# Linear attention and gated MLP, two layers on one core: queries kept token-major and turned by DMA, MLP norm from sums taken with the residual

## The chip, the core and the metric

The kernel runs on one core of a Trainium2 chip. The metric is the device time of one execution in microseconds, the median of the runs shown. PE is the matmul engine, DVE the vector engine, ACT the activation engine, POOL the GpSimd engine, and SP the engine whose queue issues nearly all DMAs.

## What is computed

The input is 2048 tokens of 512 features in bf16. Two layers follow each other with the same weights: attention, then MLP, each added to the residual x. The norm has no weights.

```
x = x + A(layernorm(x)); x = x + B(layernorm(x)); and both once more

A: q, k, v = split(x @ wqkv) into 32 heads of 16
   pq, pk  = q @ w_phi[h], k @ w_phi[h]
   phi     = concat(softmax(p), softmax(-p))            # 32 features a head
   kv, z   = sum over tokens of phi_k^T v, and of phi_k
   o       = (phi_q @ kv) / (phi_q . z + 1e-6);  result = o @ wo
B: gate = relu(x @ W_gate); up = x @ W_up; result = (gate * up) @ W_down     # F = 1376
```

## The kernel before

Tokens lie in 16 tiles of 128 rows, and x stays in SBUF as bf16 from the first load to the last store. w_phi is folded into the key and query weights at the start (`fold`), so PE computes pk and pq directly.

**Keys.** Per tile, `norm_A` takes mean and variance on DVE (L810, L811), ln and exp on ACT for the reciprocal root (L818, L820), and scales on DVE (L825). `turn` transposes the tile into `xnTA`, by DMA from SP (L787) or, for a few tiles, by PE matmuls and a copy. `Keys.begin` computes pk (L849) and v (L855), exp of +pk and -pk on ACT (L852), and sums over 16 features on DVE (L860). `Keys.finish` and `scale` turn sums into factors by ln and exp (L867, L870) and multiply two halves of 512 on DVE or GpSimd (L879). `kvz` accumulates the 65-column products of all 16 tiles in PSUM (L896). `build` then writes the masked matrix R (L918, L924).

**Queries.** `queries` computes pq feature-major, four tiles at a time (L937), and ACT writes exp(+pq) and exp(-pq) into `Eq` (L941), which is used as it lies, without a softmax sum. `attend` multiplies each of the eight groups by R with 144 columns (L955): numerators and denominators, and also the softmax sums, so that DVE can weigh both signs (L971 to L985). The result o is turned (L787 or L797), projected (L992) and added to x (L1001; L997 for the first two tiles, with the row sum).

**MLP.** `mlp` handles blocks of 1, 2 or 4 tiles: statistics (L810), centring (L1022, L1018), a turn into `xnTB`, gate and up products (L1068, and L1044 for the last 96 features), relu on ACT (L1072), a copy of up to SBUF on ACT or DVE (`evac`, L752 or L753), their product on DVE (L1076), down products (L1101), and the scaled residual (L1108).

**Order.** `op` only records operations. `plan` then places them in time by written costs, due numbers (`DUE`) and free buffers, and each engine runs its own operations in that order. `PLACE` chooses between two engines where an operation has an `alt`. Each engine's queue is in order, so an instruction that waits holds up all behind it. `idle` inserts filler matmuls on PE (L746) in gaps of the first layer's keys. Layers overlap: the keys of layer 1 start while the MLP of layer 0 still runs.

Of the kernel before, what the change touches and what calls it, by code (L numbers as in the profile page):

```python
# [8 lines left out]
P = 128  # L9
# [14 lines left out]
GE = HB * (DH + 2)  # L24
# [12 lines left out]
class Op:  # L37
    __slots__ = ("eng", "occ", "lat", "due", "emit", "deps", "takes", "uses", "start", "end", "left",
                 "then", "ready", "name", "n", "move", "spent", "port", "follow", "behind", "alt", "twin")

    def __init__(self, eng, cost, due, emit, deps=(), takes=(), uses=(), name="", move=0, port=False,
                 follow=(), alt=None):
        self.eng, (self.occ, self.lat) = eng, cost
# [35 lines left out]
FRESH = 0.77  # L79


def plan(ops):
# [11 lines left out]
    lanes = [0.0] * LANES  # L94
    open_ = {e: [o for o in ops if o.eng == e and not o.left] for e in HOP}
    order = []
    while len(order) < len(ops):
# [34 lines left out]
        if o.eng == "PE":  # L132
            warm = t + COLD if warm is None else warm
            if t < warm:
                occ, lat = 2 * occ, lat + occ
        if o.move:
            queue = max(t + 1400, queue) + o.move * (FRESH if queue < 9000 else 1.0)
            lat = max(lat, queue + 600 - t)
            lanes = lanes[1:] + [t + lat + HOP["SP"]]
        o.start, o.end, o.spent = t, t + lat, occ  # L140
# [48 lines left out]
def mm(n, cols):  # L189
    t = n * (cols / 2.4 + 2.5)  # L190
    return t, t + 170


def act(n, sbuf=False):
    return (n / 1.2 + (275 if sbuf else 64), n / 1.2 + (385 if sbuf else 170))
# [6 lines left out]
def dve(n, rate=1, more=56):  # L202
    t = n / rate / 0.96 + more
    return t, t + 98
# [7 lines left out]
RESSUM = (750, 850)  # L212
RLN, REXP = ((150, 265), (203, 318)), ((145, 262), (198, 315))
SUMS = (8 * 32.5, 8 * 32.5 + 170)
STATS = (592, 692)
SUM16 = (1140, 1225)
CENTRE, SCALE = (240, 350), (315, 410)
FILL = 216
XPOSE, XPOSE_LOADS = (1245, 3600), (1245, 3600)
RATE = 250.0  # L220


def dma(nbytes):
    return 530, 2000 + nbytes / RATE


class K:
# [9 lines left out]
    "1101000110000001001100001000100000000000010001111000011000010001110001000000000000011100100010111111"  # L237
    "1111000010110100000100000010000001100000011001011000011111100010000100001101010000001001111011010000"
    "1111100110100000010110000100000010100000010011011010100001000001001010001111110011001101111011000111"
    "1"  # L240
# [3 lines left out]
SUM_ON_PE, SPLIT, SUMMED = False, False, 2  # L244
PAIRN, PAIRK = 4, T
# [5 lines left out]
    124840698555718, 124252925051631, 124840698555715, 125332623046249, 125332623046237, 125332623044945,  # L251
    124563716811943, 124651474002544, 125330408190868, 125332623046304, 124563716811957, 126266507667699,
    125634454115563, 126229628066192, 121775727240306, 126167001450013, 126167001450460, 127129188121561,
    127129188120464, 127094235901023, 126466639653490, 130976565015723, 126315242830809, 126026073780216,
    127094235902555, 127129188121381, 126296162928321, 126296162928067, 124164240787164, 125426364192401,
    125402334135098, 125572680463274, 125519371767392, 125974726071829, 125750504763376, 125579757280012,
    125111116517781, 125262546662859, 123870973169851, 125479091639646, 125519634893654, 125402750569735,
    125720420032606, 126315242829367, 126115429498044, 125777194724969, 125402334135128, 125288327727618,
    125426364192382, 125079834957741, 125262546664085, 125297196294117, 125083742970748, 125572680463271,
    125682458895960, 125340531910116, 125650771760537, 124924227899641, 125375805988896, 125375805988747,  # L260
    125222585690632, 124164240787379, 125079834952887, 125682458896453, 125073457285470, 124441555417783,
    125262546664362, 124559450906168, 125312265963603, 125309490505260, 125650771760388, 125521196029889,
    125302414876135, 125288971855969, 125302414876075, 125319036718893, 125310924577113, 125301244472799,
    125319889098234, 125304622980711, 124441555417022, 124696086271192, 125037102060107, 125289095968268,
    125310342882178, 125097433264852, 123938863413234, 125098635011495, 125302414877679, 125298443103361,
    125302414877834, 125345179807080, 125281974922696, 125170893464912, 125310924577844, 125298773455122,
    124760528650159, 125079834956090, 124164240787032, 125519634912639, 125297196294120, 125289095970570,
    125112530384860, 124947956071454, 125087041208877, 125295339242047, 125295339242044, 125310342881683,
    125302414876836, 125563590222055, 124550413597701, 125170893460583, 125310439811694, 125310924578485,
    125310342891023, 125079834956128, 125059086062919, 125340531910042, 125288971857093, 124938480631522,  # L270
    125016964293686, 125288327733509, 125223398503866, 125345179804453, 125223398503371, 125223398503413,
    128002429020973, 125310342881575, 125004873625443, 125004873624115, 125304250990101, 125307858833262,
    126406478372943, 124715538660738, 125381551257299, 125298773455119, 125309931740009, 125034120871986,
    125223398503145, 124934003878247, 124920547621783, 125117660356287, 125304250989589, 125381551258296,
    125724846491348, 125381551257440, 125381551255756, 124974964922671, 125098650067446, 125291692659804,
    125289095968030, 125289095968469, 125345179805242, 125288327732492, 125098635010687, 125281974923160,
    125307858833059, 125223398502787, 125307858834522, 125140858237361, 126040889629027, 125223398503832,
    125364446854524, 125252231261123, 125381551257841, 125304250990712, 125381551257935, 125172912230709,
    124370185364736, 125108599924050, 125310339518705, 125302251176246, 125291692659817, 116464344164560,
    124922363544296, 125116688267329, 125108599923765, 125310109452139, 125303189236999, 125098650066178,  # L280
    125111066291136, 125026249417504, 125310339519068, 125302251175868, 125301748943397, 125307858834419,
    125262656080157, 125307858833334, 125307858831723, 125281974922936, 125016007547146, 125096908962168,
    125140858236352, 126184070097670, 126789461067573, 124985972327150, 126493631750672, 125298443105832,
    125108599921161, 125095405692172, 124194527561572, 123915330190996, 125076395401661, 125296253501352,
# [321 lines left out]
def kernel(  # L606
# [17 lines left out]
    def psum(name, n):  # L624
        return Pool([pp.tile([P, 512], F32, name=f"{name}{i}") for i in range(n)])
# [3 lines left out]
    def x_of(t):  # L629
        return X[t // C][:, t % C, :]  # L630
# [113 lines left out]
    def idle(n):  # L744
        for _ in range(n):
            nc.tensor.matmul(wps.t[:], lhsT=zero[:, 0:P], rhs=zero[:], start=True, stop=True)  # L746
# [473 lines left out]
```

## Time and profile before

| | |
|---|---|
| time, median of 3 runs | 383.84 us (383.63 to 384.19) |
| span of the profiled execution | 382.02 us |
| its own time | not given apart; median less span is 1.8 us |
| PE, DVE, ACT, POOL busy | 371.5, 311.1, 215.0, 41.9 us |
| first attention matmul of layer 0, layer 1 | 54.4, 237.5 us from the start |
| DMA | 22.83 MB, mean 60 GB/s; 188 to 232 GB/s in most slices of the first 50 us |

The instructions on an engine overlap a little at their ends, so a group's mean times its count is more than its busy time. The chain of waits gives the pace of matmuls that follow each other without a gap. A DMA's time to landing counts from its issue.

### The profile page before, as it was taken

To read this page: it belongs to the slowest core of one execution; us is meant where nothing else is said; L and a number is where in the kernel's file an instruction comes from. 1 tells how busy PE (TensorE), PEld (TensorE's weight loads), DVE (VectorE), ACT (ScalarE), POOL (GpSimd) and SP (SyncE) were. 2 spreads that over 40 slices of the span, in tenths; PEclk is the share of its full clock that TensorE was granted. 3 is DMA by queue.
4 is the path that set the end of the run, shared out by engine and by line. 5 is a ranking of instruction groups with operands and counts; after the bars stand their busy time and mean duration, and the time that the engine had idled before them with its cause. 6 is when DMAs were issued, how large, how long until landed. Compare 5 with 4: busy or idle time off the path is not lost.

```text
span 382.0 us, 7622 instructions
## 1 busy us (share of the span) xinstructions
PE 371.5 (97%) x2787; PEld 224.4 (59%) x2832; DVE 311.1 (81%) x798; ACT 215.0 (56%) x554; POOL 41.9 (11%) x44
## 2 busy tenths in 40 slices
PE   7999998999989999999999999999999999999996
PEld 4545456967545445554656654696855544467575
DVE  7999999999999989983694677999998976763334
ACT  6999989636445316772455679984526412243040
POOL 0276710000200000230020124000000000000000
PEclk9999999999999999999999999999999999999999
DMA  8497720222221321211200100013322221020110
GB/s 232 122 205 219 188 89 2 52 58 62 57 56 41 44 54 40 45 23 27 45 6 15 22 8 1 2 36 70 77 44 70 57 56 56 14 62 16 41 50 29
DMA packets 60869, 22.83 MB, mean 60 GB/s; under 512 B 52672, under 2 KB 59808, under 8 KB 60832
## 3 DMA queue, kind: packets, MB, share of 16 engines
q1 hardware_dynamic: 60416, 21.95, 24.9%
q8 instruction: 22, 0.36, 0.4%
q10 hardware_dynamic: 416, 0.39, 0.4%
q14 instruction: 15, 0.12, 0.1%
HBM read 7.91 MB, written 2.10 MB: 26 GB/s over the span
## 4 chain that ended last, share of the span: by engine, by line
PE 77%; DVE 17%; DMA 2%; issue 2%; ACT 1%; DVEq 0%
PE b L1068 31%; PE b L1101 17%; PE b L855 5%; PE b L849 5%; PE b L992 5%; PE b L937 5%; PE q L955 3%; PE b L1044 2%; PE q L896 2%; DMA xnTA<-xn 2%; DVE pr L980 1%; DVE bstA L810 1%; DVE bstB L810 1%; DVE sk L860 1%; DVE N L753 1%
## 5 line engine op out<-in xcount | busy, mean ns | idle before, releaser
L1068 PE MATMUL b<-xnTB,wgu 128*128 128x128 bf16 (+2 forms) x1191 | 152.3, 279 | 0.5
L1068 PEld LDWEIGHTS <-wgu 128*128 128x128 bf16 x1200 | 97.7, 98 | 42.5
L1072 ACT ACTIVATE gu<-b 128x512 bf16<-128x512 f32 (+1 forms) x83 | 48.0, 584 | 63.7 <-PE b L1068 61.3
L1101 PE MATMUL b<-wd,hT 128*128 128x512 bf16 (+3 forms) x349 | 82.3, 372 | 0.7
L879 POOL TENSOR_TENSOR phiK<-ek,sk 128x512 bf16<-128x512 bf16 x38 | 41.2, 1102 | 192.3 <-ACT sk L870 164.1
L1101 PEld LDWEIGHTS <-hT 128*128 128x128 bf16 (+1 forms) x363 | 34.7, 98 | 33.9 <-DVE hT L1076 0.2
L1076 DVE TENSOR_TENSOR hT<-gu 128x512 bf16<-128x512 bf16 (+1 forms) x83 | 34.0, 414 | 15.4 <-ACT gu L752 14.2
L1108 DVE SCALAR_TENSOR_TENSOR X<-b,rsB,X 128x512 bf16<-128x512 f32 (+1 forms) x33 | 23.7, 729 | 23.8 <-PE b L1101 23.8
L752 ACT CAST gu<-b 128x512 bf16<-128x512 f32 (+1 forms) x50 | 28.4, 570 | 24.0 <-PE b L1068 20.4
L860 DVE TENSOR_REDUCE sk<-ek 128x64 f32<-128x1024 bf16 x32 | 38.6, 1210 | 2.7 <-ACT ek L852 2.3
L852 ACT ACTIVATE ek<-b 128x512 bf16<-128x512 f32 x64 | 36.0, 616 | 8.3 <-PE b L849 8.1
L941 ACT ACTIVATE Eq<-b 128x512 bf16<-128x512 f32 x64 | 37.3, 629 | 3.3 <-PE b L937 3.1
L752 ACT CAST N<-q 128x384 bf16<-128x384 f32 (+1 forms) x59 | 26.1, 464 | 12.4 <-PE q L955 6.7
L855 PE MATMUL b<-wv,xnTA 128*128 128x512 bf16 x123 | 31.9, 379 | 0.3
L937 PE MATMUL b<-xnTA,Wq 128*128 128x512 bf16 x125 | 31.9, 379 | 0.2
L849 PE MATMUL b<-Wk,xnTA 128*128 128x512 bf16 x123 | 31.6, 379 | 0.4 <-DVE xnTA L753 0.2
L992 PE MATMUL b<-wo,oT 128*128 128x512 bf16 x120 | 31.3, 379 | 0.4
L753 DVE CAST gu<-b 128x512 bf16<-128x512 f32 (+1 forms) x33 | 21.8, 665 | 11.1 <-PE b L1068 11.1
L955 PE MATMUL q<-R,Eq 128*128 128x144 bf16 x256 | 27.5, 226 | 1.8 <-DVE N L753 1.3
L955 PEld LDWEIGHTS <-Eq 128*128 128x128 bf16 x256 | 20.3, 98 | 13.1 <-issue 2.6
L980 DVE TENSOR_TENSOR pr<-N,w 128x1024 bf16<-128x1024 bf16 x32 | 21.8, 683 | 0.7
L810 DVE BATCH_NORM_STATS2 bstA<-X 128x6 f32<-128x512 bf16 x32 | 21.3, 682 | 1.2 <-DMA X<-in_A_x_dram 1.0
(75 smaller groups left out, 388.9 us busy)
## 6 DMA issues: line engine op xcount, KB each, us to landing
out_dram<-X SPq DMA_DIRECT2D x15, 128.0 KB, 1.7
X<-in_A_x_dram SPq DMA_DIRECT2D x6, 256.0 KB, 3.3
wgu<-in_B_W_gate_dram SPq DMA_DIRECT2D x4, 344.0 KB, 3.4
wgu<-in_B_W_up_dram SPq DMA_DIRECT2D x4, 344.0 KB, 3.5
wd<-in_B_W_down_dram SPq DMA_DIRECT2D x5, 256.0 KB, 3.5
wv<-in_A_wqkv_dram SPq DMA_DIRECT2D x2, 256.0 KB, 4.7
wo<-in_A_wo_dram SPq DMA_DIRECT2D x4, 128.0 KB, 3.1
oT<-o SPq DMA_TRANSPOSE x28, 2.3
```

Of the source, the lines that this page charges most:

```text
L752: both = {"ACT": ("ACT", act(cols), lambda: nc.scalar.copy(out=out_(), in_=in_()), False), "DVE": ("DVE", dve(cols), lambda: nc.vector.ten ...
L849: k = op("PE", mm(4, 512), due, lambda: [nc.tensor.matmul(kp.t[:], lhsT=xnTA[c][:, b, cols], rhs=Wk2[:, b, :], start=(b == 0), stop=(b == ...
L855: v = op("PE", mm(4, 512), due_v, lambda: [nc.tensor.matmul(vp.t[:], lhsT=xnTA[c][:, b, cols], rhs=wv[:, b, :], start=(b == 0), stop=(b == ...
L860: a = op("DVE", SUM16, due, lambda: nc.vector.tensor_reduce(out=sk.t[:, row, :], in_=ek.t[:].rearrange("p g s (h f) -> p (g s h) f", f=DH) ...
L879: e.tensor_tensor(out=ph.t[:].rearrange("p g s (h f) -> p (g s h) f", f=DH)[:, lo:lo + n], in0=ek.t[:].rearrange("p g s (h f) -> p (g s h) ...
L937: q = op("PE", mm(4, 512), due(c, b), lambda b=b, qp=qp: [nc.tensor.matmul(qp.t[:], lhsT=Wq2[:, m, b * P:(b + 1) * P], rhs=xnTA[c][:, m, : ...
L941: done.append(op("ACT", act(512), due(c, b), lambda b=b, s=s, qp=qp: nc.scalar.activation(out=Eq[c][:, b, s, :], in_=qp.t[:], func=AF.Exp, ...
L955: pe.append(op("PE", mm(len(groups), GE), due, lambda ps=ps, groups=groups: [nc.tensor.matmul(ps.t[:, n * GE:(n + 1) * GE], lhsT=Eq[c][:, ...
L992: a = op("PE", mm(4, 512), due + 3, lambda: [nc.tensor.matmul(yp.t[:], lhsT=oT.t[:, b, :], rhs=wo[:, b, :], start=(b == 0), stop=(b == NB ...
L1068: nc.tensor.matmul(ps.t[:, q * W:(q + 1) * W], lhsT=wgu[:, s, b, g * P:(g + 1) * P], rhs=xT.t[:, b, 0:W], start=(b == 0), stop=(b == NB - 1))
L1072: nc.scalar.activation(out=gu.t[:, 0, 0:cols], in_=gp.t[:, 0:cols], func=AF.Relu)
L1101: nc.tensor.matmul(yp.t[:, 0:c1 - c0], lhsT=h.t[:m, f * W + i * P:f * W + (i + 1) * P], rhs=wd[:m, f, c0:c1], start=(f == 0), stop=(f == N ...
```

## The change

- Queries are computed token-major, one tile at a time (`query`), with the transposed norm as stationary operand. They get the softmax factors that keys get (sum, ln, exp, two halves), and the finished tile of 128x1024 is turned by one DMA from SP into `fq`.
- `attend` multiplies `fq` by an R of 68 columns a group; numerators and denominators come out directly, in one PSUM buffer of two banks. A reciprocal (or ln and exp on ACT) and one product from PSUM give o.
- Halves of keys are written in place, and a pool of 23 buffers serves keys and queries. GpSimd may also scale xn.
- The residual after attention always takes row sums; sums of squares (ACT or DVE) replace the MLP's batch statistics, with four small steps for the factor.
- The product of gate and up may read up straight from PSUM.
- All x tiles are loaded ahead of the four weight transposes; wo is loaded with other rows.
- `plan` has other costs for DMAs and lets an instruction fetch of PE delay a DMA in flight; `DUE` and `PLACE` are new. So the order on every engine differs.

The diff, cut to its core (the tables, the recording of R's two writes and most of the costs are left out):

```diff
-GE = HB * (DH + 2)
+GE = HG * (DH + 1)
...
         if o.move:
-            queue = max(t + 1400, queue) + o.move * (FRESH if queue < 9000 else 1.0)
-            lat = max(lat, queue + 600 - t)
+            start = max(t + 1220, queue)
+            queue = start + o.move * (FRESH if start < 9000 else 1.0)
+            lat = max(lat, queue + 390 - t)
...
-    p_q, p_b = psum("q", 2), psum("b", 6)
+    p_q, p_b = psum("q", 1, [NG, P]), psum("b", 6, [512])
-    p_ek, p_phi = pool("ek", 4, [NG, 2, GQ]), pool("phiK", 4, [NG, 2, GQ])
+    p_ek = p_eq = pool("ek", 23, [NG, 2, GQ])
+    p_fq, p_rd = pool("fq", 8, [NG, P]), pool("rd", 3, [H], F32)
...
-        first_x(6, 2)])
+        first_x(6, 2), first_x(8, 2), first_x(10, 2), first_x(12, 2), first_x(14, 2)])
...
+            b = op("DVE", SCALE, due, lambda scaled=scaled: scaled(nc.vector), [a], [xn], name="xnA", port=2,
+                   alt=("POOL", (800, 850), lambda scaled=scaled: scaled(nc.gpsimd), 3))
...
-    def queries(c, due, xT, after):
...
+    def query(l, t, due, xT, behind, key):
+        qp, ek, sq, fq = Buf(p_a), Buf(p_eq), Buf(p_sq), Buf(p_fq)
+        q = op("PE", mm(4, 512), due, lambda: [nc.tensor.matmul(
+            qp.t[:], lhsT=xnTA[c][:, b, cols], rhs=Wq2[:, b, :], start=(b == 0), stop=(b == NB - 1))
+            for b in range(NB)], [xT] + q_fold, [qp, ek], name="Q", follow=key)
+        e = [op("ACT", act(512), due, lambda s=s: nc.scalar.activation(
+            out=ek.t[:, :, s, :], in_=qp.t[:].rearrange("p (g e) -> p g e", e=GQ), func=AF.Exp, scale=1.0 - 2.0 * s),
+            [q], (), [qp, ek], name="Eq") for s in range(2)]
+        a = op("DVE", SUM16, due, lambda: nc.vector.tensor_reduce(
+            out=sq.t[:], in_=ek.t[:].rearrange("p g s (h f) -> p (g s h) f", f=DH), axis=AX.X, op=Alu.add),
+            e, [sq], [ek], name="sq", follow=behind)
...
+        a = halves("phq", ek, lambda: ek.t[:], lambda lo, n: sq.t[:, lo:lo + n], PHI["POOL"], due, [a], [], [ek, sq])
+        a = op("SP", XWIDE, due, lambda: nc.sync.dma_start_transpose(
+            out=fq.t[:], in_=ek.t[:].rearrange("p g s e -> p (g s e)")), a, [fq], [ek], name="fq", move=1450)
+        return fq, a
...
+        pe = [op("PE", SUMS, due, lambda: [nc.tensor.matmul(
+            ps.t[:, g, 0:GE], lhsT=fq.t[:, g, :], rhs=R[:, g, :], start=True, stop=True) for g in range(NG)],
+            [ready] + made, [ps], [fq], name="erq")]
...
+        a = op("DVE", dve(512), due, lambda: nc.vector.tensor_tensor(
+            out=o.t[:].rearrange("p (g j d) -> p g j d", g=NG, d=DH),
+            in0=ps.t[:, :, 0:GQ].rearrange("p g (j d) -> p g j d", d=DH),
+            in1=rd.t[:].rearrange("p (g j) -> p g j", g=NG).unsqueeze(3).to_broadcast([P, NG, HG, DH]),
+            op=Alu.mult), [a], [o], [ps, rd], name="o")
...
-            a = stats(l, "B", t, due_x(i), [after[t]])
-            seen.append(a)
...
+            seen.append(op("ACT", SQUARE, due_x(i), lambda t=t: nc.scalar.activation(
+                out=wasteA[:], in_=x_of(t), func=AF.Square, accum_out=ssq[:, l, t:t + 1]), [after[t]], name="ssq",
...
+            def direct(up=up, gu=gu, cols=cols, f0=f0):
+                nc.vector.tensor_tensor(out=h.t[:, f0 * W:f0 * W + cols], in0=gu.t[:, 0, 0:cols], in1=up.t[:, 0:cols],
+                                        op=Alu.mult)
```

## The prediction, made before the changed kernel was run

> **What bounds the kernel now.** I read the page's busy shares first, then the windows view cut at the two places where PE starts on the attention of a layer, then the chain, then the groups by form, last the timeline around one GpSimd half.
>
> ```profile
> PE 371.5 (97%) x2787; PEld 224.4 (59%) x2832; DVE 311.1 (81%) x798; ACT 215.0 (56%) x554; POOL 41.9 (11%) x44
> ```
> ```profile
> 0.00:54.40 54.40, 51.76 (x378) 26.67 (x386) 50.34 (x105) 48.40 (x132) 23.91 (x28) 1.00 0.72 185
> 54.40:237.00 182.60, 178.99 (x1302) 107.69 (x1324) 154.05 (x389) 105.05 (x271) 17.95 (x16) 1.00 0.17 34
> 237.00:382.00 145.00, 140.76 (x1108) 90.08 (x1122) 106.76 (x306) 61.51 (x154) 0.00 (x0) 1.00 0.19 45
> ```
>
> The columns after each stretch are its length and the busy time of PE, PEld, DVE, ACT and POOL. PE is busy nearly everywhere, at a granted clock of 1.00. A busy PE may still wait, so I count what it streams. The chain merges equal matmuls and so gives their pace:
>
> ```profile
> 51.73 0.80 PE q L896 x24
> 350.52 4.70 PE b L1101 x21
> 362.15 0.89 PE b L1068 x16
> 240.18 0.86 PE b L937 x4
> ```
>
> That is 0.033 us for 65 columns, 0.22 for 512 (0.216 by L937: 0.86/4) and 0.056 for 128; in the same view eight of 256 take 0.87 (0.109 each), sixteen of 192 (L1044) take 1.48 in the timeline with a tail of some 0.14 (0.084), and three of 144 start 0.19 before the next instruction (0.0625). With the counts of the program's PE stream this is 49.5 us before the first L955 (at 54.4 in the timeline), 179.2 up to the first L955 of layer 1 (237.5) and 141.1 after it: 369.8 of 382.0. Only 4.9, 3.9 and 3.4 us are not streaming. PE's own work is the bound in all three stages, with DVE close behind in the first (50.3 of 54.4).
>
> The costs that matter come from these groups, and from one clash in the timeline:
>
> ```profile
> L955 PE MATMUL q<-R,Eq 128*128 128x144 bf16 x256 | 27.5, 226 | 1.8 <-DVE N L753 1.3 <-DVE R L924 0.3 <-DVE R L918 0.2
> L860 DVE TENSOR_REDUCE sk<-ek 128x64 f32<-128x1024 bf16 x32 | 38.6, 1210 | 2.7 <-ACT ek L852 2.3 <-issue 0.3
> L980 DVE TENSOR_TENSOR pr<-N,w 128x1024 bf16<-128x1024 bf16 x32 | 21.8, 683 | 0.7
> L753 DVE CAST gu<-b 128x512 bf16<-128x512 f32 x31 | 21.0, 681 | 11.1 <-PE b L1068 11.1
> ```
> ```profile
> 102.53 1.06 POOL L879 TENSOR_TENSOR phiK<-ek,sk 128x512 bf16<-128x512 bf16 x1 [0.41 <-ACT sk L870]
> 102.66 0.98 DVE L973 TENSOR_TENSOR m<-m 128x32 f32<-128x32 f32 x1
> ```
>
> L973 takes 0.205 on average; here it starts inside a GpSimd half and ends with it, 0.78 late.
>
> **PE.** Queries, K, V, projection and MLP keep their matmul counts. Only the 256 matmuls against R shrink from 144 to 68 columns: 256 x (0.0625 - 0.0345) = 7.2 us less, 0.0345 being the 65-column pace scaled by 68/65. By the busy time of L955 (27.5 us, waits and tails included) the saving would be nearer 19; I take the streaming figure because the chain shows what lies behind each matmul starting at that pace. The instruction order shows 19 filler matmuls (idle, L746) instead of 13: 6 x 0.216 = 1.3 more. It also puts 14 instead of 13 blocks of queries ahead of the first attention. The streams become 51.6, 175.7 and 136.7: 364.0 in all, 5.8 less.
>
> **DVE.** Instruction means overlap: all groups sum to 360.6 us against 311.1 busy over 798 instructions, 0.062 each, which I take off every instruction. Gone per tile are m, den, w (0.21 each), pr (0.683), the bf16 sum o (0.413), its share of the N and DS copies, and stats B (0.68 + 0.17). New per tile are the sum sq (1.21 by L860) and o straight from PSUM (0.681, by the f32 cast of L753). Residual sums cost 0.67 + 0.08 for 0.67 before; 13 sums of squares 0.76 each; the norm 60 small steps at 0.155 instead of 30; 17 reciprocals (0.342) instead of 32; 39 second factors are multiplied out of PSUM (0.68), so 33 casts fall away; 36 halves instead of 26 (0.703). With the order's counts: 50.5 before R of layer 0, 135.4 between the two Rs, 88.8 after, against 49.7, 153.4 and 108.2 by the same sum (the windows say 50.3, 154.1, 106.8). DVE loses 36 us, all of it behind the first stage, where PE has the longer sum: worth nothing by itself, but it removes rivals for the end.
>
> **ACT** loses the N and DS copies and part of ru, and gains ln and exp for the queries (0.28 each), 15 pairs for the denominators and 19 squares (0.6 to 0.7): 215 becomes about 211. Hidden under PE. If squares needed another activation table, each change would cost 1.28 (the one load in the page); the order has no second load, so I take zero.
>
> **GpSimd** goes from 38 halves to 92, plus 14 scaled xn, for which no row exists: between 0.40 (DVE's row) and 1.06 (a half of the same size). I take 1.06 as the row of its own engine. 106 x 1.06 = 112 us, hidden except in the first stage. There the order puts 32 halves and 3 xn between the first K half and the last one: 35 x 1.06 = 37.1. The first half started at 15.66; DVE's first sum now stands 0.9 earlier, so 14.8. Without clashes: 51.9. Meanwhile DVE runs 7 xn (0.38) and 5 halves (0.66) that cannot share time with a GpSimd half as in the clash above: 6.0 more, 57.9. The last sums against vext, R and hops (0.26 + 0.3 + 0.9, with a query block between, 0.86) would put the first attention matmul at 60.3 if all of it is serial. DVE's own sum puts it at 50.5 + 3.4 start-up + 0.9 = 54.9, PE's at 51.6 + 4.9 = 56.5. I take **57**, nearest to PE's sum, since before also ended its first stage by PE's sum; ends 54.9 and 60.3.
>
> **DMA.** 32 transposes of 128x1024 come to the SP queue. The nearest rows are those of 128x512: 1.19 to issue, 2.3 to 4.3 to landing. Twice the size bounds the issue by 1.19 and 2.38, the landing by 2.3 and 5.5 (two in a row, 1.19 + 4.3). On SP, 38 to 76 us of issue join some 120 of transposes: no bound over 380 us. The eight in a row after the weights serve the first tiles. For the third, PE reaches its matmul 3.6 us of work and about 2.5 us of chain after the first, while four more halves (4.2) and a landing (2.7 typical) less the 1.3 of R give 5.6 against 6.1: just in time, late by 1.1 at a landing of 4.3. The PE queue is in order, so projections and MLP wait behind it; I put such lateness at 0, with 0 to 3 us for both layers in the range.
>
> One PSUM buffer of two banks now serves all R matmuls, so the next tile's wait until o has read the last: 0.45 + 0.34 + 0.68 and hops, 1.5 us. The order keeps 1.7 us or more of PE work between them except twice near the start (1.4): 0.2 at most. Loads of wo by other rows move the same bytes, for nothing.
>
> The four late x loads move ahead of the four weight transposes: 4 x 0.58 = 2.3 us on SP and 1 MB at 225 GB/s, 4.7 us, on the engines. These delay the fold of Wq; the order puts that fold and every query behind more K and V tiles, which cover it. Without that cover the start loses up to 4.7. The norm's four small steps on DVE stand before resB only; down (10 us per block) hides them.
>
> **Sum.** 57 + (175.7 + 3.9) + (136.7 + 3.4) = 376.7, keeping today's idle time of the later stages because their chains are as long or shorter (the first tile loses m, den, w, pr and copies, about 1.9 us, but waits on a DMA). Around the span lies 383.84 - 382.02 = 1.8 us, so **378.5** against 383.84.
>
> **Rivals.** First, DVE was the real drag on the later stages: with 36 us less of it, the stages start at 54.9 and lose only about 2 us each: 54.9 + 177.7 + 138.7 + 1.8 = 373.1. For it: DVE's windows of 154 in 183, and waits of PE on N and R in L955's row. Against: 3.9 and 3.4 us is all there is to win.
>
> Second, slower: GpSimd and DVE block each other in the first stage. With 0.78 lost by each of the 12 DVE operations there, on DVE's own sum, 54.9 + 12 x 0.78 = 64.3, and 64.3 + 179.6 + 140.1 + 1.8 = 385.8. It decides against the change from 63.1 on, at 0.68 per operation. For it: the clash shown, halves of up to 1.56 and an xn of 1.22 (median 0.34) in the views by line; GpSimd is now wanted for nearly all of the stage. Against: the mean of DVE's halves (0.703) lies only 0.045 above its least (0.658), although GpSimd was busy 23 us of that stage. The Trainium skill (SBUF — State Buffer, "Who interferes with whom") has this as a rule: DVE and GpSimd share a port pair by an exclusive lock, and an operation with two SBUF inputs blocks fully, whoever came first going on. The clash above agrees with it, 0.98 instead of 0.205. By the rule in full every overlap is serial, the 60.3 end and 381.8 in all; without it the stage would end by DVE's or PE's sum, 376.4 to 378.0.
>
> Third, no change: the 5.8 us come back as waits on transposed queries, 0.18 per tile over 32 tiles, 384 in all. The page of before cannot show it, as its Eq came from ACT without a DMA.
>
> **Chances.** About 0.2% (0.77 us) is what a measurement can tell here, so faster means under 383.1. The forecast has 0.58, the first rival 0.19: faster 0.77. No change 0.07, slower 0.16. The range runs from 373.0, the first rival, to 385.5, almost the second: it takes in 60.3 for the first stage (381.8) and 3 us of late transposes on top.
>
> **What would show it.** Right: the R matmuls at 0.035 pace, first one near 57, layer 1's near 236.6, PE still 96 to 97% busy, DVE near 275 of busy time, POOL near 112. Wrong: PE waiting for DMA fq in sums above 3 us, a first attention later than 60, halves above 1.2 on average, or ACT with more than one table load.

## The result and the profile after

The changed kernel takes 393.8 us (393.1 to 394.7) against 383.8, a ratio of 1.0258 with a 95% interval of 1.0242 to 1.0274. The forecast was 378.5 with a range of 373.0 to 385.5; even the slower rival's 385.8 was too low. The profiled execution took 393.77 us with a span of 392.0, so 1.8 us lie around the span as before, and spans compare directly.

First the page's busy line, then the windows view of the changed kernel, cut where PE starts on the attention of a layer (at 62.63 and 245.85):

```profile
PE 370.1 (94%) x2792; PEld 217.6 (56%) x2838; DVE 287.5 (73%) x581; ACT 212.6 (54%) x564; POOL 131.5 (34%) x112
```
```profile
0.00:62.63 62.63, 56.54 (x388) 29.00 (x396) 55.21 (x94) 52.15 (x146) 48.47 (x46) 1.00 0.70 169
62.63:245.85 183.22, 176.35 (x1303) 103.28 (x1324) 141.74 (x277) 101.10 (x276) 68.05 (x54) 1.00 0.31 57
245.85:392.00 146.15, 137.21 (x1103) 85.36 (x1118) 90.59 (x211) 59.31 (x144) 14.96 (x14) 1.00 0.38 69
```

The three stages take 62.6, 183.2 and 146.2 us where the forecast has 57.0, 179.6 and 140.1: 5.6, 3.6 and 6.1 too long, 15.3 in all. Against the streams of 51.6, 175.7 and 136.7, PE idles 11.0, 7.5 and 9.5 us, where before it idled 4.9, 3.9 and 3.4. PE's clock is 1.00 throughout.

Next the groups that the prediction priced, from the groups by form (busy time and mean ns of one, then idle time before them and what ended it):

```profile
L598 POOL TENSOR_SCALAR xn<-X,mvA,rsA 128x512 bf16<-128x512 bf16 x14 | 29.5, 2110 | 67.2 <-ACT rsA L592 58.3 <-ACT rd L728 5.0 <-DVE bstA L582 3.7
L598 DVE TENSOR_SCALAR xn<-X,mvA,rsA 128x512 bf16<-128x512 bf16 x18 | 9.7, 550 | 4.0 <-ACT rsA L592 3.3 <-DMA xnTB<-xn 0.4 <-DMA xnTA<-xn 0.3
L612 POOL TENSOR_TENSOR ek<-ek,sk 128x512 bf16<-128x512 bf16 x50 | 55.0, 1123 | 49.9 <-ACT sk L662 25.9 <-DVE bstA L582 14.7 <-DVE hT L831 6.9
L612 DVE TENSOR_TENSOR ek<-ek,sk 128x512 bf16<-128x512 bf16 x14 | 12.1, 861 | 0.7 <-ACT sk L662 0.7
L765 DVE SCALAR_TENSOR_TENSOR zero<-X 128x512 bf16<-128x512 bf16 x13 | 10.7, 823 | 0.0
L734 DVE TENSOR_TENSOR o<-q,rd 128x512 bf16<-128x512 f32 x32 | 21.8, 682 | 3.0 <-ACT rd L731 2.7
L724 PE MATMUL q<-R,fq 128*128 128x68 bf16 x256 | 13.4, 194 | 0.6 <-DVE o L734 0.3 <-DMA fq<-ek 0.2
```

The row that did not exist before now does: the scaled xn takes **2.11 us on GpSimd**, where the same line on VectorE takes 0.55, and a GpSimd half of the same size takes 1.12. VectorE's 36 halves (14 of keys at 0.861, 22 of queries at 0.737, together 0.785) and its squares (0.823) take more than the 0.703 and 0.76 forecast, while o from PSUM takes the 0.68 forecast. The matmuls against R wait for fq for 0.2 us only.

The timeline around the first two GpSimd xn (start, duration, engine, line; in brackets the idle time before it and what ended it) shows how their length reaches PE:

```profile
12.60 4.14 POOL L598 TENSOR_SCALAR xn<-X,mvA,rsA 128x512 bf16<-128x512 bf16 x2 [11.29 <-ACT rsA L592]
16.70 4.15 POOL L612 TENSOR_TENSOR ek<-ek,sk 128x512 bf16<-128x512 bf16 x4
16.76 2.03 SPq L556 DMA_TRANSPOSE xnTA<-xn  x1
18.87 0.43 PE L674 MATMUL q<-vext,ek 128*128 128x65 bf16 x8 [0.72 <-POOL ek L612]
```

The transpose of the second xn and the first halves of the keys both start when it ends, at 16.74, and PE waits 0.72 us for these halves. With all xn on VectorE (an experiment below) the same transpose starts at 14.41, the halves at 15.21, and the same matmuls at 17.70 without a wait. Not every wait behind an xn is the xn's: PE's longest wait for xnTA, 1.07 us at 107.15, has its transpose behind others on SP's queue, and with that xn on VectorE it is still 0.81. And here two VectorE halves stand beside GpSimd ones, 1.25 and 1.54 us long instead of some 0.68:

```profile
51.98 2.07 POOL L612 TENSOR_TENSOR ek<-ek,sq 128x512 bf16<-128x512 bf16 x2
...
53.35 1.25 DVE L612 TENSOR_TENSOR ek<-ek,sq 128x512 bf16<-128x512 bf16 x1
54.44 3.55 POOL L612 TENSOR_TENSOR ek<-ek,sk 128x512 bf16<-128x512 bf16 x3 [0.39 <-ACT sk L662]
54.53 1.54 DVE L612 TENSOR_TENSOR ek<-ek,sk 128x512 bf16<-128x512 bf16 x1
```

I laid every VectorE instruction of the trace against GpSimd's and compared those that overlap a GpSimd instruction with the median of the same kind that do not. Halves, squares, xn, xc and the small steps m2 and ve are longer beside GpSimd (halves 3.8 us in all, xn 2.5, squares 1.9, xc, the centring ahead of the MLP, 1.7, ve 1.7, m2 1.3); reduces, statistics and everything that reads PSUM (o, the residual sums, copies, second factors) are not. Over all kinds, those that come out a little shorter included, it is 12.3 us.

Last, SP's queue, which the prediction set aside. Its issues in a part of the stretch behind the first attention, from the timeline of the changed kernel:

```profile
86.16 1.26 SPq L716 DMA_TRANSPOSE fq<-ek  x1
87.51 1.24 SPq L556 DMA_TRANSPOSE oT<-o  x1
88.84 1.26 SPq L716 DMA_TRANSPOSE fq<-ek  x1
90.20 1.24 SPq L556 DMA_TRANSPOSE oT<-o  x1
91.53 1.19 SPq L841 DMA_TRANSPOSE hT<-hr  x1
92.81 2.38 SPq L716 DMA_TRANSPOSE fq<-ek  x1
```

There is no gap of more than 0.1 us. Summed over the trace (issues that start in the stretch), SP issues for 43.3 us of the stretch from 62.6 to 112, and again for 43.4 us from 245.9 to 300; in the kernel before it was 22.5 of the 49.6 us from 54.4, and 24.7 of the 53.5 from 237.5.

### The profile page after: what moved, and what is told of

Its sections match the earlier page's. It is cut to its first block, busy times and chain, and to the rows that moved or that the text cites. A ratio compares the mean times of both kernels' runs of the same rounds, so it can differ in the third digit from the quotient of the medians.

```text
span 392.0 us, 7563 instructions
## 1 busy us (share of the span) xinstructions
PE 370.1 (94%) x2792; PEld 217.6 (56%) x2838; DVE 287.5 (73%) x581; ACT 212.6 (54%) x564; POOL 131.5 (34%) x112
## 4 chain that ended last, share of the span: by engine, by line
PE 55%; DVE 20%; ACT 8%; issue 7%; POOL 5%; DMA 3%; SPq 1%; DVEq 0%; POOLq 0%; ACTq 0%
PE b L814 29%; PE b L854 13%; PE b L740 4%; DVE sq L708 3%; POOL xn L598 3%; ACT ek L705 3%; PE b L639 2%; DVE o L734 2%; POOL ek L612 2%; DVE ek L612 2%; DVE bstA L582 2%; PE b L790 2%; PE b L645 2%; ACT ek L642 2%; DVE X L744 2%
## 5 line engine op out<-in xcount | busy, mean ns | idle before, releaser
L854 PE MATMUL b<-wd,hT 128*128 128x512 bf16 (+2 forms) x345 | 82.5, 372 | 1.9 <-ACT sq L713 0.5
L612 POOL TENSOR_TENSOR ek<-ek,sk 128x512 bf16<-128x512 bf16 x50 | 55.0, 1123 | 49.9 <-ACT sk L662 25.9
L612 POOL TENSOR_TENSOR ek<-ek,sq 128x512 bf16<-128x512 bf16 x42 | 46.8, 1136 | 39.5 <-PE b L814 13.4
L598 POOL TENSOR_SCALAR xn<-X,mvA,rsA 128x512 bf16<-128x512 bf16 x14 | 29.5, 2110 | 67.2 <-ACT rsA L592 58.3
L642 ACT ACTIVATE ek<-b 128x512 bf16<-128x512 f32 x64 | 35.1, 598 | 12.6 <-PE b L639 12.5
L831 DVE TENSOR_TENSOR hT<-gu,b 128x512 bf16<-128x512 bf16 (+1 forms) x39 | 26.2, 674 | 20.7 <-PE b L814 20.5
L708 DVE TENSOR_REDUCE sq<-ek 128x64 f32<-128x1024 bf16 x32 | 38.0, 1207 | 0.2
L705 ACT ACTIVATE ek<-b 128x512 bf16<-128x512 f32 x64 | 35.8, 631 | 0.0
L833 ACT CAST gu<-b 128x512 bf16<-128x512 f32 (+1 forms) x44 | 24.7, 561 | 17.4 <-PE b L814 17.0
L702 PE MATMUL b<-Wq,xnTA 128*128 128x512 bf16 x125 | 30.7, 379 | 0.2
L734 DVE TENSOR_TENSOR o<-q,rd 128x512 bf16<-128x512 f32 x32 | 21.8, 682 | 3.0 <-ACT rd L731 2.7
L744 DVE SCALAR_TENSOR_TENSOR X<-b,X 128x512 bf16<-128x512 f32 x32 | 21.7, 679 | 2.3 <-PE b L740 2.0
(73 smaller groups left out, 378.5 us busy)
```

Of the source, the lines that this page charges most:

```text
L598: e.tensor_scalar(out=xn.t[:], in0=x_of(t), scalar1=mv[:, t, 0:1], scalar2=rs[:, t:t + 1], op0=Alu.subtract, op1=Alu.mult)
L612: e.tensor_tensor(out=out().rearrange("p g s (h f) -> p (g s h) f", f=DH)[:, lo:lo + n], in0=ek.t[:].rearrange("p g s (h f) -> p (g s h) f ...
L642: e = [op("ACT", act(512), due, lambda s=s: nc.scalar.activation(out=ek.t[:, :, s, :], in_=kp.t[:].rearrange("p (g e) -> p g e", e=GQ), fu ...
L705: e = [op("ACT", act(512), due, lambda s=s: nc.scalar.activation(out=ek.t[:, :, s, :], in_=qp.t[:].rearrange("p (g e) -> p g e", e=GQ), fu ...
L708: a = op("DVE", SUM16, due, lambda: nc.vector.tensor_reduce(out=sq.t[:], in_=ek.t[:].rearrange("p g s (h f) -> p (g s h) f", f=DH), axis=A ...
L854: nc.tensor.matmul(yp.t[:, 0:c1 - c0], lhsT=h.t[:m, f * W + i * P:f * W + (i + 1) * P], rhs=wd[:m, f, c0:c1], start=(f == 0), stop=(f == N ...
```

## The experiments

There were two theories to begin with, and a third from the trace. **Theory 1**: xn on GpSimd, mis-sized by a factor of two. **Theory 2**: GpSimd's halves, by the port that they share with VectorE and by their length. **Theory 3**: the transposes of the queries, on SP's queue or by their landing. In the edits, code put behind `order = arrange(ops)` changes an instruction's engine and leaves its place in the order. "The order" is what the kernel's planner laid out.

**The instructions alone.** Runs of one form on GpSimd, and then on VectorE, each behind the other, with no layer around them (two of the ten calls):

```
run(pool=[(xn, 6), (xsub, 6), (ximm, 6), (half, 6), (mul, 6)])
run(dve=[(mul, 1), (xn, 6), (xc, 6), (half, 6), (mul, 6), (small, 6), (reduce, 6), (mul, 1)])
```

> This kernel computes none of the layers: it loads x, runs GpSimd and VectorE instructions of the sizes in question alone and then side by side, and stores x unchanged. Theory 1 (the scaled xn is dear on GpSimd by itself): the 128x512 bf16 xn of L598's form takes about 2.07 us on an idle chip, with VectorE waiting, and a half 1.03 to 1.06. If the price goes by arithmetic step, the subtract-only form takes about 1.0, if by operand it stays near 2. Theory 2 (shared port): alone it takes about 1.06 as the half does, and 2.07 only beside VectorE work. For VectorE beside back-to-back halves theory 2 expects xn (0.35 alone), half and product of two bf16 tiles (0.41 alone) and the 4-element product to be stretched to the period of a half, 1.0 to 1.1, and a reduce of 1.2 not at all.

The groups by form of that run, GpSimd's xn, half, xn with constants in place of the two per-row operands, and xn with the subtraction alone:

```profile
L71 POOL TENSOR_SCALAR pa<-X,mv 128x512 bf16<-128x512 bf16 x70 | 145.0, 2072 | 6.2
L80 POOL TENSOR_TENSOR pa<-X,sc 128x512 bf16<-128x512 bf16 x112 | 118.1, 1055 | 8.0
L77 POOL TENSOR_SCALAR pa<-X 128x512 bf16<-128x512 bf16 x12 | 23.1, 1923 | 1.0
L74 POOL TENSOR_SCALAR pa<-X,mv 128x512 bf16<-128x512 bf16 x12 | 18.7, 1561 | 1.1
```

So 2.07 is what the instruction costs by itself, with VectorE idle; theory 1's price holds. A second arithmetic step costs 0.51, so the price goes neither by the step nor by the operand alone (1.0 or 2 expected, 1.56 measured), and the form with one tile as input is dearer than the half with two (a product of two bf16 tiles took 1.15). On VectorE by itself xn took 0.41, xc 0.35, the half 0.69, the product 0.42, the 4-element product 0.16 and the reduce 1.22. The pairs meant to run side by side waited for each other in this kernel, so theory 2 was not tried by it.

**The instructions side by side.** The same with the two engines started together:

> The instructions by themselves again, with none of the layers computed: 12 GpSimd halves (or 8 scaled xn) against a run of one VectorE form, this time started together. (In the first such kernel the two engines' stretches waited for each other, so it showed only the lone durations: half 1.05, xn 2.07 on GpSimd.) Theory of the shared port: VectorE's xn (0.41 alone), xc (0.35), half (0.69), product of two bf16 tiles (0.42) and 4-element product (0.16) can't run inside a GpSimd instruction; beside halves they start or end at a half's end, so that several per half aren't had and their period comes near 1.1 to 1.5; beside GpSimd's xn 2.1 or more. The reduce stays at 1.22. Rival: the stretched instructions of the trace have another cause (semaphores, SBUF banks of the same tile); then the periods stay within 10% of the lone ones: xn 0.45, xc 0.39, half 0.73, product 0.46, small 0.20.

VectorE's groups of that run: half, reduce, xn, 4-element product, product of two tiles, xc. Each mean is over all its partners, GpSimd's halves and, but for the last two, its xn:

```profile
L80 DVE TENSOR_TENSOR da<-X,sc 128x512 bf16<-128x512 bf16 x48 | 52.9, 1102 | 1.5
L97 DVE TENSOR_REDUCE red<-X 128x64 f32<-128x1024 bf16 x40 | 48.8, 1219 | 1.2
L71 DVE TENSOR_SCALAR da<-X,mv 128x512 bf16<-128x512 bf16 x48 | 39.9, 831 | 1.6
L92 DVE TENSOR_TENSOR sm<-sm 128x4 f32<-128x4 f32 x96 | 36.7, 382 | 3.2
L84 DVE TENSOR_TENSOR da<-X 128x512 bf16<-128x512 bf16 x24 | 28.1, 1169 | 0.8
L87 DVE TENSOR_SCALAR da<-X,mv 128x512 bf16<-128x512 bf16 x24 | 26.1, 1090 | 0.8
```

Beside back-to-back halves alone, as the median or typical value of each stretch:

| VectorE form | alone | beside GpSimd halves | the halves meanwhile |
|---|---|---|---|
| xn 128x512 | 0.41 | 1.10 | 1.06 |
| xc 128x512 | 0.35 | 1.10 | 1.06 |
| half 128x512 | 0.69 | 1.43 | 1.38 |
| product of two bf16 tiles | 0.42 | 1.16 | 1.12 |
| product of 4 elements | 0.16 | 0.16 and 0.91 in turn | 1.06 |
| reduce 128x1024 | 1.22 | 1.22 | 1.06 |

The clash is there, and its price is the rest of the half that is running, about 0.7, for every VectorE form but the reduce; of the 4-element products every second one pays it. The rival (10%) is out. Beside GpSimd's xn the theory was wrong: it expected 2.1 or more for VectorE's xn there, and the trace has 0.41 to 0.83, and 0.69 to 1.18 for the half, so a GpSimd xn, 2.1 to 2.6 us long then, holds VectorE up for a part of its time only. The Trainium skill (SBUF — State Buffer, "Who interferes with whom") states that an exclusive lock on a shared port pair decides this and that a reduce never contends; the table agrees in the first five rows and in the last. By its full exclusion a pair of halves would need 0.69 + 1.05 = 1.74, and here the pair came every 1.46; an xn and a half would need 0.41 + 1.05 = 1.46, and came every 1.13. So in this case the blocking was not complete.

**All xn back on VectorE.**

```
+    for o in ops:
+        if o.name == "xnA" and o.eng == "POOL":
+            o.swap()
```

> All 14 scaled xn back on VectorE, in the same places of the order; all else as after. Theory 1 (xn on GpSimd at 2.07 instead of the 1.06 bounded from the halves is the main loss): the first attention comes back from 62.6 to 58 or 59, both later stages lose 2 us each, and the time is 385.8 (384 to 388). Theory 2 (the clash of GpSimd's halves with VectorE is the main loss): the 14 xn come under the same halves on VectorE, 0.4 to 0.8 each, and the time stays at 391 or above. Theory 3 (transposes on the SP queue): 392 or above.

388.7 us (388.0 to 389.2), ratio to before 1.0128 (1.0112 to 1.0145): 5.1 us of the 10.0 are gone, fewer than theory 1's 8, and the time is 0.7 above its range. The stages are 59.8, 181.1 and 145.3, so the first two gained 2.8 and 2.1 and the last, which has no xn, 0.9. Theory 1 has half of the loss against the kernel before, and a third of the 15.3 us to the forecast.

**Only the first layer's five xn back.** The same edit over the first 16 xn.

> Only the five scaled xn of the first layer back on VectorE; the nine of the second layer stay on GpSimd. Theory 1: the first attention at 58 to 59 as with all 14, and about half of the gain of all 14: 389.5 (388 to 391). Theory 2 or 3: 392.5 or above, the first attention within 1 us of 62.6.

391.1 us (391.0 to 391.8), ratio 1.0191 (1.0175 to 1.0206): 2.7 gained, and the first attention comes at 60.1, within 0.3 of where it is with all of them back. So five xn in the first stage cost 2.7 and the nine of the second layer 2.4; 0.5 and 0.3 each, of the 1.66 by which a GpSimd xn is longer.

**The kernel before, with 14 xn on GpSimd.** The same tiles, the same places (the edit is cut to its core).

```
+    on_pool = (2, 4, 9, 10, 14, 16, 17, 19, 21, 23, 24, 26, 28, 30)
+    for n, o in enumerate([o for o in ops if o.name == "xnA"]):
+        if n in on_pool:
+            o.swap()
```

> The kernel before with only this added: the xn of the same 14 tiles are scaled on GpSimd instead of VectorE, in the same places of its order. GpSimd has 38 halves there instead of 92, so an xn queues less. Theory 1: 2.07 instead of 0.40 before a transpose that K or V waits for, 14 x 1.67 = 23 us at most, of which the part that K waits for is lost: 388 to 392, the first attention later than 54.4 by 2 to 4 us. Theory 2 or 3: 384 to 385.5, as the GpSimd work is off the path.

389.3 us (389.0 to 389.6), ratio 1.0139 (1.0124 to 1.0154): 5.3 us slower than the kernel before beside it (384.0), with the first attention at 57.0 instead of 54.4. The single cost, put into the good kernel, comes out as it did when taken from the changed one.

**GpSimd's halves cut to one head.**

```
-                    "POOL": ("POOL", (1016, 1058), lambda k=k: phi(nc.gpsimd, k * H, H), 3)}
+                    "POOL": ("POOL", (1016, 1058), lambda k=k: phi(nc.gpsimd, k * H, 1), 3)}
```

> The kernel with all xn on VectorE (388.7), with every GpSimd half cut from 32 heads to one head, so that 15 sixteenths or more of GpSimd's work and of its port time are gone while each wait stays. (The other heads are left unscaled.) The trace of that kernel holds 13.2 us of VectorE time above the same forms' lone durations while a GpSimd half runs. Theory 2 as second cause (GpSimd's halves, by their length and by the clash): the first attention moves from 59.8 to about 55, and the time comes to about 379 to 382, near the forecast. Theory 3 (transposes on the SP queue hold the rest): 386.5 or above.

382.5 us (381.6 to 383.6), ratio 0.9967 (0.9955 to 0.9978): 6.2 below the 388.7, half a us above theory 2's range. The overlapping VectorE instructions show no excess any more. But the gain is spread: the first stage gets 1.7 of it (58.1, not 55), the second 2.0, the last 2.4. The edit takes away the clash and the length of the halves together; this run does not part them.

**Queries copied instead of transposed.** `dma_start` for `dma_start_transpose` in the issue of fq.

> The kernel with all xn on VectorE (388.7), with the 32 transposes of scaled queries (1.23 us of issue each on SP, landing after 3.0 to 5.1) replaced by plain copies of the same bytes (queries stay token-major, so the result is not attention; 0.57 of issue by the x loads' rows). Theory 3 (SP's queue and the slow landing of transposes hold the rest): 382 to 385. Theory 2: within 1.5 us of 388.7, as PE waited for fq for 0.9 us only.

384.9 us (384.1 to 386.2), ratio 1.0023 (1.0013 to 1.0034): 3.8 below the 388.7, inside theory 3's range. The first stage does not move (59.9), the second gains 1.4 and the last 2.6, the two stages in whose first 50 us SP's queue was nearly full. PE's waits for fq itself were 0.9 us, so most of what was gained must be the other tiles' wait behind these transposes.

**All three at once.**

> All three suspected costs taken away at once from the changed kernel: xn on VectorE, GpSimd's halves cut to one head of 32 (the others left unscaled), queries copied instead of transposed (left token-major). Singly they gave 5.1, 6.2 and 3.8 of 393.8. If they add up: 378.7, the forecast's 378.5, and nothing else of size is left. If halves and transposes hide behind each other: 381 or above. If PE's streams were not 5.8 us shorter than before, it can't come below 381 either.

378.2 us (378.0 to 379.1), ratio 0.9855 (0.984 to 0.987). The windows view:

```profile
0.00:58.06 58.06, 54.57 (x395) 27.53 (x396) 53.00 (x99) 51.50 (x146) 9.11 (x43) 1.00 0.72 189
58.06:235.70 177.64, 176.21 (x1325) 103.75 (x1324) 137.97 (x286) 101.69 (x276) 10.59 (x44) 1.00 0.24 57
235.70:376.40 140.70, 137.23 (x1120) 85.61 (x1118) 87.34 (x211) 59.23 (x144) 2.88 (x11) 1.00 0.28 72
```

The costs add up: 5.1 + 6.2 + 3.8 = 15.1, and together 15.6. The span of 376.4 is 12.4 above the 364.0 of streams, against 12.2 in the kernel before. So the time agrees with the sum of PE's streams, and what the forecast lacked is of the size of these three costs. By stage the agreement is looser: 6.5, 1.9 and 4.0 us over the streams, where the kernel before has 4.9, 3.9 and 3.4. And this kernel leaves out nearly all the work of GpSimd's halves, which the forecast counted as work that hides. That the total meets the forecast within 0.3 us is in part luck.

**Queries transposed from ScalarE's queue.**

> The kernel with all xn on VectorE (388.7), with the 32 transposes of scaled queries issued from ScalarE's queue instead of SP's, in the same places of the order. With plain copies on SP instead the time was 384.9. Theory 3a (the 1.23 us that each transpose takes on SP's queue delay the transposes of xnTB, oT and xnTA behind them): 385 to 387, less some 1 us for ScalarE's other work behind a 1.2 us issue. Theory 3b (the landing of the transposes and the DMA engines' time are what counts): no gain, 388.5 or above.

445.6 us, ratio 1.1611 (1.1588 to 1.1635). This does not tell 3a and 3b apart, since something else came in: in the timeline three oT issues on SP stretch over 9.38 us, with an issue of ScalarE's queue in the middle. The third line is from the view of SP's own waits (sum, times, longest):

```profile
74.04 9.38 SPq L556 DMA_TRANSPOSE oT<-o  x3
77.93 1.25 ACTq L716 DMA_TRANSPOSE fq<-ek  x1
SPq L556 <- DMA fq<-ek: 119.6, 22, 24.7
```

One by one the three issues take 1.19, 1.26 and 1.19 us; the rest is a wait on semaphores. SP's transposes wait for the landing of an fq 22 times, for 119.6 us in all, a wait that the kernel with all transposes on SP does not have, and ScalarE's queue stops in the same way on the semaphores of SP's transposes. So in this program the two queues' transposes take turns, each after the other's landing. This and the granted clock, 0.95 on average in that run, go with the 57 us more; how much each makes is not shown.

**The copies issued in two parts each.**

> The kernel with all xn on VectorE and the queries copied instead of transposed (384.9), each copy now cut into two of half the size (queries stay token-major): two issues of 0.57 make 1.14, near the 1.26 of a transpose, while the bytes are the same and the landing stays near 2.4 to 3. Theory 3a (SP's queue time): back to 387.5 to 389. Theory 3b (the transpose's slower landing, or its use of the DMA engines): stays at 384.5 to 386.

386.3 us (385.8 to 387.0), ratio 1.0070 (1.0053 to 1.0086): between the two theories. An issue took 0.55 (median) here and 0.47 when the copy was whole, so SP's queue got 1.10 - 0.47 = 0.63 more per tile, and the time 1.4 us. A transpose takes 1.26, 0.79 more than the whole copy; in proportion that makes 1.8 of the 3.8. By this one step, and if the price is in proportion, about half is SP's time. The other half would go with the landing (3.3 against 2.4 or less) or the load of the DMA engines; the runs do not part these two.

**All halves on GpSimd, and the last stage's on VectorE.** The first moves VectorE's 36 halves to GpSimd. The second, which also has the squares on ScalarE, moves the GpSimd halves that the order has behind the second layer's first attention to VectorE; the trace shows 13 moved of the 14 expected.

> The kernel with all xn on VectorE (388.7), with VectorE's 36 halves moved to GpSimd too, which then does all 128. Side by side, a half took 1.43 on VectorE against 0.69 alone and 1.38 on GpSimd against 1.05, so this takes away the dearest clash and 27 us of VectorE's time. Theory 2a (the clash is what the halves cost): 386 to 387.5. Theory 2b (the length of GpSimd's halves in the chain from sum to transpose or key sum is what they cost, 1.05 for 0.69 and in a row instead of in parallel): 389 to 392.

> All xn on VectorE and all sums of squares on ScalarE (387.7), and the GpSimd halves behind the first attention of the second layer (14, 15.0 us of GpSimd) moved to VectorE, which is busy for 90 of 145 us there. Nothing is left out. With these halves cut the last stage was 2.5 us shorter (145.3 to 142.8). If their price there is GpSimd's length and clash: 385 to 386.5. If it is their place in the chain whichever engine has them: 387.5 or above.

396.7 us (395.1 to 397.1) for the first, ratio 1.0340 (1.0323 to 1.0357), 8.0 slower than 388.7 though the clash of VectorE's halves is gone and VectorE's busy time is 15 us less. The clash as a whole is not gone: by the comparison used above it rose from some 13 to some 17 us, since GpSimd's longer work now meets the centring ahead of the MLP (6.5 us of it). And one wait stands out: PE stands still for 4.5 us for a centring, and from 60.6 to 80 the granted clock is 0.91, worth some 1.8 us (an estimate, 0.09 x 19.4). 390.4 (390.1 to 391.4) for the second, ratio 1.0175 (1.0160 to 1.0190), 2.7 slower than the 387.7 that it started from, though the clash fell there by some 3 us. Neither theory of a gain held; the first run is even above its rival's 389 to 392, the second inside its rival's 387.5 or above. This fits a half that is in the chain on either engine, where the engine that gets more of them gets later with all that stands behind. How much of the 6.2 is clash and how much the length of the halves, these runs do not part.

**Squares on ScalarE.**

> The kernel with all xn on VectorE (388.7), with VectorE's 13 sums of squares moved to ScalarE, which does the other 19 and is busy for 55% only. On VectorE they took 0.874 on average, up to 1.54 beside a GpSimd half, 0.684 alone. Theory 2a (clash): VectorE loses 11.4 us, the norm's scale comes earlier, 387 to 388. Theory 2b: no change within 0.7, or slower by the ScalarE queue's wait of 0.82 per square.

387.7 us (387.5 to 388.3), ratio 1.0101 (1.0086 to 1.0116), 1.0 less than with xn on VectorE alone; of theory 2 that is the part that squares have. It is the fastest kernel tried that leaves nothing out, and is still slower than before.

**The order made anew.** If the losses came from an order laid out on wrong prices, a new order on right ones should recover them. The squares on VectorE got the port too, and `DUE` and `PLACE` were replaced, by other lists in each of the two kernels (the edit is cut to its core).

```
-                   alt=("POOL", (800, 850), lambda scaled=scaled: scaled(nc.gpsimd), 3))
+                   alt=("POOL", (2040, 2072), lambda scaled=scaled: scaled(nc.gpsimd), 3))
-            name="m2")
+            name="m2", port=True)
-            [r] + seen, name="ve")
+            [r] + seen, name="ve", port=True)
```

> The changed kernel with its order made anew by its own planner: all xn on VectorE, and the sums of squares and the two first steps of the norm (m2, ve) entered as users of the port that GpSimd holds, as measured side by side; due times and places (which engine has which half, square, denominator or second factor) are changed to suit, 91 halves on GpSimd instead of 92. Nothing is left out. Theory: the losses are not in the operations but in an order that was laid out on wrong prices (0.80 for an xn of 2.07, and norm steps without the port), so that every late step hits the next one; then the time falls below before, to 379 to 383 (378.2 was had with halves and transposes gone). Rival: GpSimd's halves and the transposes cost their 6.2 and 3.8 in any order: 386 to 389.

> The same, but with twelve of the 32 scaled xn on GpSimd, entered at 2.07 instead of 0.80, and 84 halves there. Theory (the price in the order, not the engine, was wrong): within 1.5 us of the other redone order, though two seconds of GpSimd per xn stay. Rival (GpSimd is the wrong engine for xn, as 14 of them cost 5.1 in the changed order and 5.3 in the kernel before): slower than the other redone order by 4 us or more.

(In the second text, "two seconds" stands for two us.) 392.3 us (391.8 to 392.5), ratio 1.0219 (1.0205 to 1.0233), and 390.0 (389.1 to 391.0), 1.0171 (1.0157 to 1.0184). The theory fell: neither came below 386, and the first is above its rival's 386 to 389 too. The excess beside GpSimd did fall, from 12.3 to 6.3 and 5.3 us, but PE now waits elsewhere. PE's waits of the first of the two, longest sums first (sum, times, longest; its L783 is the projection, L682 K and L688 V):

```profile
PE b L783 <- DMA oT<-o: 6.4, 4, 1.9
PE b L682 <- DMA xnTA<-xn: 2.5, 4, 1.6
PE b L688 <- DMA xnTA<-xn: 1.8, 2, 1.3
```

The transposes that PE waits for came late, probably because single clashes were left (an xn of 1.26, an m2 of 1.03) and because SP's queue was as full as before (42 of 49 us behind the first attention); neither was taken away by itself. The rival of the second kernel fell as well: with twelve xn on GpSimd at their true price it was 2.3 us faster than the one with none. The two have different lists, so the 2.3 is not the price of the xn alone. It shows that an order with twelve xn on GpSimd need not be slower than one with none, and suggests that the 5.1 is the price of xn in an order that counts on 0.80. Whether any order brings the changed kernel below 383.8 stays open.

## Why the prediction was wrong, point by point

The steps that failed are three terms of the sum: the GpSimd xn, taken at 1.06 us; GpSimd's halves, taken as hidden but for the first stage; and SP's queue, taken as "no bound". The runs showed 5.1, 6.2 and 3.8 us for them, 15.1 of the 15.3 by which the time missed the forecast.

**PE's streams** (364.0, 5.8 less than before) agree with the runs: with the three costs out, 12.4 us are left over them, and 12.2 before. A block of eight matmuls against R takes 0.42 us in the timeline, 8 x 0.0345 and the tail of 0.14. The 378.5 was the time of a kernel in which nothing new waits.

**GpSimd's xn** is the term that was mis-sized. I bounded it by 0.40 and 1.06 and took the half as "the row of its own engine"; it costs 2.07. The half was a row of the right engine and the wrong form, so it was no bound from above. 14 x 1.05 = 14.7 us more, and 0.07 more for each of 92 halves, make 112 into some 133, and the page has 131.5. Its share of the time is 5.1, its clash with VectorE and its place in this order included.

**GpSimd's halves and DVE.** DVE was to lose 36 us and be busy for 275; it was busy for 287.5, and 275 + 12.3 of clash is 287.3. With the halves cut it was busy for 279.0, of which the 14 xn that it had taken over make some 6. The step that failed is that I took the 112 us of GpSimd as hidden in the later stages and counted the clash for the first stage only, at 0.5 us for each of 12 instructions, though GpSimd's halves reach into both later stages: cut, they gave 2.0 and 2.4 there and 1.7 in the first. And "all of it behind the first stage ... hidden" was read off averages over 183 us. In the 49 us behind the first attention DVE is as full as before, from the windows views of the changed kernel and of the kernel before:

```profile
62.63:112.00 49.37, 45.15 (x462) 31.37 (x467) 47.30 (x105) 28.44 (x86) 25.51 (x22) 1.00 0.67 117
```
```profile
54.40:104.00 49.60, 47.96 (x460) 34.42 (x465) 48.35 (x151) 31.29 (x91) 2.12 (x2) 1.00 0.21 44
```

47.30 of 49.37 us after, 48.35 of 49.60 before: the DVE time saved lies in the late, slack stretches, and the clash falls where none is left. PE is not busy for 4.2 of these 49.4 us, against 1.6 of 49.6 before.

**DMA**: "no bound over 380 us" was right for the 380 us and wrong for these stretches, where SP issued for 43 of 49 and of 54 us. The same windows show the DMA engines at 0.67 for 0.21. The waits for fq were 0.7 us, within the 0 to 3 forecast; what was overlooked is who stands in SP's queue behind fq: oT, xnTB and xnTA, for which PE does wait. The price is 3.8; whether SP's time or the slower landing makes it is open, about half each by the one run that bears on it.

**The first stage** came at 62.6, beyond the 60.3 that I gave as its end if all is serial. 2.8 of the 5.6 is xn, 1.7 the halves; 1.1 is left. **ACT** (212.6 for 211, one table load), the one PSUM buffer (0.3 for at most 0.2) and the norm's small steps cost about what was said, but for the steps m2 and ve, which the clash lengthened by 3.0 in all. The late x loads were not tried by themselves.

**Rivals.** The second had the right sign and one of the mechanisms, the halves beside VectorE. Its 64.3 for the first stage is near the measured 62.6 by luck: the halves were worth 1.7 there and the xn, which it did not have, 2.8. It gave 385.8 since it kept the later stages whole: in them the clash, SP and the second layer's xn cost 9.7 against the forecast. The first (DVE as drag) and the third (0.18 of waiting per tile on fq) did not occur in that form. The chance of 0.77 for faster rested on the forecast and a rival that both assumed that what is off the path on average is off it everywhere.

## What to carry to other kernels

Price an operation that moves to another engine by a row of that engine *and that form*; where none exists, measure it alone, since it can be twice the nearest row (here 2.07 for 1.05). Ask for each queue and engine how full it is in the 50 us in which PE's next work is made, not over the kernel: SP at 88% and VectorE at 96% there left no room, which 50% and 73% over the span hid. In a tight order each late step can make the next one late: moving halves either way, or redoing the order, gained nothing here.

## What the runs showed of the hardware that was not expected

On GpSimd a 128x512 bf16 subtract-and-multiply by two per-row operands takes 2.07 us, with constants 1.92, the subtraction alone 1.56, while a product with a broadcast f32 tile takes 1.05 and one of two bf16 tiles 1.15: the form with fewer tiles to read is the dearer. The Trainium skill (GPSIMD Engine Reference, "4.1 Engine selection") has it the other way, with one-input forms at roughly line rate and two-input ones some twice as slow; beside VectorE's 0.41 and 0.69 for xn and half alone, the measured ratios are 5.0 and 1.5, and the measurement decides. A VectorE product of 4 elements per row, 0.16 alone, takes 0.91 when it meets a GpSimd half; all forms but the reduce lose about 0.7, so in proportion the smallest lose the most. The issue of a 128x1024 transpose takes 1.23 to 1.26 and that of 128x512 1.19, so between these two sizes SP pays by the instruction and hardly by the size, but single issues took 2.0 to 2.6. Transposes issued from two queues waited for each other's landing on the program's semaphores, for 119.6 us of SP's time in one run.
